# An mLSTM block and a rational feed-forward on one core: first gates by themselves, constants ahead of the branch, a new order of the work, the last step in halves

## The chip, the cores and the metric

The kernel runs on one core of one Trainium2 chip. The metric is the device time of one execution in microseconds (us). Lower is better.

## The reference

Two stages follow each other. The first is an mLSTM over 4 batches, 8 heads, 768 tokens and a head dimension of 40; the second sends the 3072 rows of 320 values through a feed-forward with 2048 hidden values and a rational activation. All inputs are 32-bit floats except the weights, which reach the device as 64-bit floats.

```python
for t in range(S):                       # S = 768
    m_new  = max(f_gate[t] + m, i_gate[t])
    f_stab = exp(f_gate[t] + m - m_new)
    i_stab = exp(i_gate[t] - m_new);  m = m_new
    C = f_stab * C + i_stab * outer(v[t], k[t])
    n = f_stab * n + i_stab * k[t]
    y[t] = sigmoid(o_gate[t]) * (C @ q[t]) / max(abs(n @ q[t]), 1)
h = x @ w_in                             # x = y, tokens by 320
P = a0 + a1*h + a2*h**2 + a3*h**3
Q = 1 + abs(b0)*abs(h) + abs(b1)*h**2
out = (P / (Q + 1e-6)) @ w_out
```

## The kernel before, in words

**Branch.** `_can_square` (line 233) loads the four numbers `moe_a`, decides on VectorE (DVE) whether the cubic can be written with a square, and reads the answer into registers. `tc.If` then runs one of two copies of `_program`. Here it is the copy with `square=True`.

**Gates.** `gates()` loads all of `f_gate` and `i_gate` (32 rows of 768), finds the running maximum with one scan, subtracts it, computes the exponential with 14 DVE instructions on tiles of 128x384, and multiplies the forget gates up in chunks of 64 tokens. The results go to DRAM: `scrF` (the gates themselves) and `scrA` (their products). Both are written in four quarters of three chunks each (`store_f`, `store_a`, lines 420 to 432), the first quarter at once and the other three when the order says so. The input gates are turned by TensorE (PE) into `inat`.

**Attention.** `attention(u)` handles unit u, 128 tokens of one batch: unit u has block n = u // 4 and batch b = u % 4. Units 0 to 3 are the first 128 tokens of the four batches, unit 4 the next 128 of batch 0. There are 24. A unit loads k and q (`ld`: tiles kr, qn), v (`lv`: vb) and its gates, spread over 64 partitions (`lg`: fb from scrF, ab from scrA). Its chain is: kp (k by gates, GpSimd, called POOL), tk and tq (transposes into kq on PE, copied by ScalarE, called ACT, to kT and qb), sc (the scan e on DVE), qA and P (pm, on DVE), then on PE S (ps), ow, it and i1 (y), then na, gt, xn, and a transpose px that ACT and DVE split into a high and a low part, xk.

**Weights.** w_in comes in eight slabs i0 to i7 and two slabs j0, j1, w_out in eight slabs o0 to o7. `split64` turns 64-bit floats into two 32-bit parts. Each slab needs two ACT passes (raw, z), two DVE passes (raw, z), a high part on ACT and a subtraction on POOL (wi, wo, wY).

**Feed-forward.** `feed_forward(n, i)`: two units make a block n of 256 tokens (12 blocks); step i of 8 handles 256 hidden values. f1 (16 matmuls into ph), then ha, u and p on ACT, w = w*ha on POOL, p on DVE, y and r0 on ACT, gH and m (w) on DVE, rm (p - w) on POOL, gL on DVE, and on PE f2 (gH by wo, 8 matmuls) and f3 (gL by wo, 4 matmuls) into the two tiles po. Step 7 of a block ends with two evictions ot and their DMAs to the output.

**Order.** Nothing is issued where it is written. Every operation is put into `_Plan` with a key, a cost, what it reads and what it writes; `_Plan.order()` plays the list forward and, on each engine, takes the ready operation with the smallest key. The keys come from the tables `FFN_AT`, `ATT_AT`, `PREP_AT`, `SLAB_AT` and others. `_Ordered` then ties each engine to that order, and all DMAs go through SyncE's (SP) queue. Instructions of one engine run in this order and wait at the head of the queue. `busy()` adds 90 matmuls `hot` whose result nobody reads.

Since nearly every instruction is issued by the recording helper at line 33, the trace is read by tiles (ps, y, po) rather than by lines.

## Time and profile before

| what | value |
|---|---|
| three timed runs | 578.12 us median, 577.51 to 578.72 |
| profiled execution, its own time | 580.5 us |
| span of that execution, first to last instruction | 578.6 us |
| granted TensorE clock, mean over the span | 0.957 of full |
| PE busy | 520.7 us (90%), 180 of its matmul rows are `hot` |
| DVE busy | 465.1 us (80%) |
| ACT busy | 430.6 us (74%) |
| POOL busy | 380.8 us (66%) |
| chain that ended last | PE 69%, DVE 5%, ACT 4% |

The table averages over stages with different limits. The timeline in 40 slices shows PE busy at nine tenths or more from the eleventh slice to the thirty-eighth, and mostly at less in the ten slices before; so the views by stage matter more than the shares. The profiled execution took 580.5 us, 1.9 us above its span and 2.4 us above the median of the timed runs.

### The profile page before, as it was taken

How to read it: one execution, taken by the hardware profiler on the slowest of the kernel's cores; microseconds unless marked ns; L12 is line 12 of the kernel's file. 1: busy time of each engine (PE TensorE's matmuls, PEld its weight loads, DVE VectorE, ACT ScalarE, POOL GpSimd, SP SyncE). 2: the span in 40 equal slices, each digit the busy share in tenths (PEclk: the TensorE clock that was granted, in tenths of full speed). 3: DMA queues.
4: the chain of work that ended last, by engine and by line, in shares of the span. 5: the costliest groups of instructions: out<-in, count | busy, mean ns of one | idle time of the engine just before them, and what ended most of it. 6: DMA issues, size and time to landing. Idle time of an engine off the chain costs nothing.

```text
span 578.6 us, 13044 instructions
## 1 busy us (share of the span) xinstructions
PE 520.7 (90%) x5023; PEld 488.8 (84%) x5023; DVE 465.1 (80%) x753; ACT 430.6 (74%) x751; POOL 380.8 (66%) x350
## 2 busy tenths in 40 slices
...
GB/s 91 309 177 174 240 216 147 93 66 48 77 77 49 83 65 62 85 63 56 80 54 65 84 42 84 76 53 72 53 49 44 6 1 24 1 24 2 23 1 30
DMA packets 120521, 44.06 MB, mean 76 GB/s; under 512 B 103746, under 2 KB 112962, under 8 KB 120450
## 3 DMA queue, kind: packets, MB, share of 16 engines
...
q14 instruction: 30, 0.25, 0.1%
...
## 4 chain that ended last, share of the span: by engine, by line
PE 69%; DVE 5%; ACT 4%; issue 2%; POOL 1%; DVEq 0%; ACTq 0%; POOLq 0%
PE ph L33 27%; PE po L33 26%; PE y L33 6%; PE ps L33 4%; PE kq L33 3%; PE ow L33 2%; PE px L33 2%; ACT ph L33 1%; DVE w L33 1%; DVE gH L33 1%; POOL p L33 1%; DVE gL L33 1%; DVE p L33 1%; ACT p L33 1%; ACT kT L33 0%
## 5 line engine op out<-in xcount | busy, mean ns | idle before, releaser
L33 POOL TENSOR_TENSOR p<-p,w 128x512 f32<-128x512 f32 x96 | 127.1, 1324 | 113.4 <-DVE w L33 108.0
L33 PE MATMUL ph<-xk,wi 128*128 128x256 f32 x1152 | 174.3, 286 | 1.7 <-DVE gL L33 1.7
L33 PEld LDWEIGHTS ph<-xk,wi 128*128 128x128 f32 x1152 | 152.6, 189 | 4.4 <-issue 2.3
L33 POOL TENSOR_TENSOR w<-w,ha 128x512 f32<-128x512 f32 x96 | 131.2, 1368 | 13.9 <-ACT w L33 12.8
L33 PE MATMUL po<-wo,gH 128*128 128x320 f32 x768 | 140.0, 318 | 0.0
L33 PEld LDWEIGHTS po<-wo,gH 128*128 128x128 f32 x768 | 115.4, 190 | 4.8 <-issue 2.7
L33 DVE SCALAR_TENSOR_TENSOR gH<-p,ps,ph 128x512 fp32r<-128x512 f32 x96 | 71.2, 741 | 24.8 <-ACT ph L33 19.8
L33 DVE SCALAR_TENSOR_TENSOR gL<-p,ps,ph 128x512 fp32r<-128x512 f32 x96 | 70.4, 733 | 24.6 <-POOL p L33 23.8
L33 DVE SCALAR_TENSOR_TENSOR w<-w,gH 128x512 f32<-128x512 f32 x96 | 81.4, 847 | 4.4
L33 ACT ACTIVATE w<-ha,ba 128x512 f32<-128x512 f32 x96 | 78.1, 814 | 6.2
L33 ACT ACTIVATE ph<-w,cd 128x512 f32<-128x512 f32 x96 | 66.0, 688 | 18.0 <-DVE p L33 11.2
L33 ACT ACTIVATE ha<-ph 128x512 f32<-128x512 f32 x96 | 57.2, 596 | 29.1 <-PE ph L33 29.0
L33 PE MATMUL po<-wo,gL 128*128 128x320 f32 x384 | 73.7, 313 | 4.2 <-DVE gL L33 4.1
L33 DVE SCALAR_TENSOR_TENSOR p<-p,ps,ph 128x512 f32<-128x512 f32 x96 | 71.0, 741 | 3.1 <-ACT p L33 2.1
L33 PEld LDWEIGHTS po<-wo,gL 128*128 128x128 f32 x384 | 60.0, 189 | 7.4 <-DVE gL L33 6.8
L33 ACT ACTIVATE p<-ph,ps 128x512 f32<-128x512 f32 x96 | 65.3, 680 | 0.3
L33 ACT ACTIVATE ph<-ph 128x512 f32<-128x512 f32 x96 | 55.9, 582 | 3.0
L33 PE MATMUL ph<-xk,wj 128*128 128x256 f32 x192 | 54.1, 282 | 0.0
L33 PE MATMUL ph<-xk,wY 128*128 128x256 f32 x192 | 54.0, 281 | 0.0
L33 DVE TENSOR_TENSOR_SCAN e<-fb,eye 128x512 f32<-128x512 f32 x24 | 40.8, 1699 | 0.2
L33 PE MATMUL ps<-qb,kT 104*64 104x128 f32 x384 | 28.9, 298 | 10.9 <-DVE qA L33 10.3
L33 PEld LDWEIGHTS ph<-xk,wj 128*128 128x128 f32 x192 | 36.5, 190 | 0.0
(108 smaller groups left out, 762.1 us busy)
## 6 DMA issues: line engine op xcount, KB each, us to landing
...
```

The lines of the kernel that those rows point to most:

```text
L33: made = fn(*args, **kwargs)
```

## The change

**Ahead of the branch.** A new `_prologue` makes the constants that both copies need (identity, `cd`, the cleared kp, qn0, vb0 and qb) and loads the gates of the first 128 tokens of all 32 rows (`ef`, `ei`, 32x128) before the answer of the branch is known.

**First gates.** A new `early()` repeats the gate computation on these 128 tokens: 27 instructions on DVE, one transpose on PE, two copies on ACT, and three DMAs into chunks 0 and 1 of scrF and scrA. Units 0 to 3 wait for these alone (`=scrF`, `=scrA`, `=inat0`). The large `gates()` still runs over all 768 tokens; its key is now `GATE_AT`, its first quarter stores only chunk 2, and `spread` leaves out the first column block.

**Last step.** With `HALVED = 1` the activation work of the very last step (block 11, step 7) is done in two halves of 256 columns each, and the second of the last two evictions runs on DVE.

**Order.** All tables are new, each operation can have its own offset (`NUDGE`, some 620 entries), and the planner's engines start at 3.6 to 4.1 us rather than 0.6 to 2.0. The first 24 `hot` matmuls have a cost of 0.45 instead of 0.22, and the first waits for the early gates' subtraction rather than for a point inside the large exponential.

```diff
+def _prologue(ctx, tc, args):
+    c = {name: pool.tile(shape, F32, name=name) for name, shape in (
+        ("ident", [P, P]), ("cd", [P, 1]), ("kp", [P, H, L]), ("qn0", [P, H, L]), ("vb0", [P, H, 2, D + 1]),
+        ("qb", [D + L, H // 2, 2, 2, L]), ("ef", [BH, 2 * L]), ("ei", [BH, 2 * L]),
+    )}
+    c["flag"] = _can_square(ctx, tc, args[8])
+    for t, src in ((c["ef"], args[4]), (c["ei"], args[3])):
+        nc.sync.dma_start(t, src.rearrange("b h s -> (b h) s")[:, 0 : 2 * L])
+    nc.vector.memset(c["kp"], 0.0)
+    nc.vector.memset(c["vb0"], 0.0)
+    make_identity(nc, c["ident"])
+    nc.gpsimd.memset(c["cd"], CD)
+    nc.gpsimd.memset(c["qn0"], 0.0)
+    nc.gpsimd.memset(c["qb"], 0.0)
+    return c
...
+    def early():
+        step(clear, 0.13, w=["em", "ep"], new=new)
+        step(lambda: V.tensor_tensor_scan(m[:, 1:], ef, ei, -1e30, op0=ALU.add, op1=ALU.max), 0.35, w=["em"])
+        step(lambda: V.tensor_tensor(f, ef, m[:, 0:C], ALU.add), 0.2, w=["em"])
+        step(less, 0.37, r=["em"], w=["ex.f", "ex.i", "mark"])
+        exp(
+            lambda fn, r, w, **kw: step(fn, r=["ex.f", "ex.i", "ep"], w=["ex.f", "ex.i", "ep"], **kw),
+            dict(gx=x, gt=t, gm=mm, gr=r, gp=p),
+        )
+        step(turn, 0.12, "PE", r=["ex.i"], w=["pe"], new=[("pe", ("a", 1))])
+        step(spread, 0.37, "ACT", r=["pe"], w=["inat0"])
+        step(firsts, 0.13, w=["ex.f", "ep"])
+        step(lambda: V.tensor_tensor_scan(a, x[:, 0:L], a0, 0.0, op0=ALU.mult, op1=ALU.add), 0.2, r=["ex.f"], w=["ep"])
+        plan.add("gate", FIRST - 1, "SP", 0.5, store_f, r=["ex.f"], w=["scrF"], lag=2.1)
+        plan.add("gate", FIRST - 1, "SP", 1.0, store_a, r=["ep"], w=["scrA"], lag=2.1)
...
-            key = FIRST - 1 if j == 0 else STORE_AT + j
+            key = STORE_AT + j
...
-        scr = [f"=scr{j}" for j in sorted({2 * n // CQ, (2 * n + 1) // CQ})]
+        scr = [f"=scr{j}" for j in sorted({2 * n // CQ, (2 * n + 1) // CQ})] if n else ["=scrF", "=scrA"]
...
+        last = NS * n + i >= NS * NU // 2 - HALVED
+        cuts = [slice(j * T, (j + 1) * T) for j in range(2)] if last else [slice(0, W)]
...
-        def f_w():
-            nc.gpsimd.tensor_tensor(d["w"], d["w"], d["ha"], op=ALU.mult)
+        def f_w(c):
+            nc.gpsimd.tensor_tensor(d["w"][:, c], d["w"][:, c], d["ha"][:, c], op=ALU.mult)
...
+            if engine == "DVE":
+                nc.vector.tensor_scalar(ot, po, pa[:, 3:4] if square else 1.0, None, op0=ALU.mult)
```

In the table of offsets a row reads like `S_0=40.63, ke_0=-15.75, P_0=11.71, ow_0=914.85`, one number for each operation of each unit or step.

**What the order does, first place: SP and PE from the branch to unit 0.** Names carry the unit or slab: kr0 is unit 0's k, rawi2 slab i2. On SP before, from the first load after the branch (unit 0's v, k and q stand ahead of the weights):

```order
L388 DMA gate_f_148<-in_f_gate_dram 32x768
L389 DMA gate_i_149<-in_i_gate_dram 32x768
L392 DMA pa_107<-in_moe_a_dram 128x4
L393 DMA pb_108<-in_moe_b_dram 128x2
L636 DMA vb0_118<-in_v_dram 64x8x40 x2
L630 DMA kr0_185<-in_k_dram 128x8x40
L631 DMA qn0_115<-in_q_dram 128x8x40
L630 DMA kr1_189<-in_k_dram 128x8x40
L528 DMA rawj0_200<-in_moe_w_in_dram 64x1024
```

On SP now, some rows after the branch:

```order
L720 DMA rawi2_215<-in_moe_w_in_dram 128x2x512
L720 DMA rawo0_225<-in_moe_w_out_dram 128x2x640
L528 DMA scrF_133<-early_kT_168 64x64
L532 DMA scrA_134<-early_qA_169 32x64 x2
L720 DMA rawi1_253<-in_moe_w_in_dram 128x2x512
L837 DMA fb0_265<-scrF_133 64x512 x2
L843 DMA ab0_266<-scrA_134 64x2x256 x2
L1077 DMA og0_285<-in_o_gate_dram 128x8x40
L837 DMA fb1_289<-scrF_133 64x512 x2
L843 DMA ab1_290<-scrA_134 64x2x256 x2
L1077 DMA og1_310<-in_o_gate_dram 128x8x40
L822 DMA kr0_315<-in_k_dram 128x8x40
```

The first gates are now written behind one j slab, two i slabs and one o slab, where before eight slabs had been issued; unit 0's k and q stand behind them, and its v (vb0) twelve rows further down, behind j1, i3, o3 and o1. On PE now, the first rows after the branch:

```order
L34 MATMUL hot_194<-ident_58 128x128 x11
L34 MATMUL pe_232<-ident_58,early_kT_168 64x64
L34 MATMUL hot_194<-ident_58 128x128 x59
L34 MATMUL kq0_396<-ident_58,kp_60 104x128 x4
L34 MATMUL hot_194<-ident_58 128x128 x8
L34 MATMUL kq0_424<-ident_58,qn0_61 104x128 x4
L34 MATMUL hot_194<-ident_58 128x128 x12
L34 MATMUL ow_0_476<-vb0_62,pm0_410 40x82 x8
L34 MATMUL ps_0_513<-qb_63,kT0_413 64x128 x8
```

All 90 `hot` matmuls now stand ahead of unit 0's ow; before, they were spread out down to unit 2's.

**Second place: DVE around P of unit 4**, the first unit that needs the large gates (pm4 is P, e4 the scan, p0_1 step 1 of block 0). Before:

```order
L33 TENSOR_TENSOR qA4_1028<-kq4_1010,ab4_963 104x512
L33 SCALAR_TENSOR_TENSOR e4_1036<-fb4_962,eye_106 128x512
L33 SCALAR_TENSOR_TENSOR zi5_1038<-zi5_1038,rawi5_722 128x512
L33 SCALAR_TENSOR_TENSOR zo5_1051<-zo5_1051,rawo5_796 128x640
L33 SCALAR_TENSOR_TENSOR rawi7_832<-rawi7_832 128x512
L33 TENSOR_TENSOR pm4_1065<-ps_4_1040,e4_1036 128x8x64
```

Now, with what follows it:

```order
L34 SCALAR_TENSOR_TENSOR e4_1027<-fb4_920,eye_127 128x512
L34 SCALAR_TENSOR_TENSOR zo5_1036<-zo5_1036,rawo5_703 128x640
L34 TENSOR_TENSOR qA4_1054<-kq4_1029,ab4_921 104x512
L34 TENSOR_TENSOR xn3_1064<-y_3_944,gt3_1034 128x320
L34 SCALAR_TENSOR_TENSOR p0_1_1062<-p0_1_1062,ps_130,ph0_1_876 128x512
L34 SCALAR_TENSOR_TENSOR zi7_1076<-zi7_1076,rawi7_809 128x512
L34 TENSOR_TENSOR pm4_1052<-ps_4_1067,e4_1027 128x8x64
L34 SCALAR_TENSOR_TENSOR p0_2_1079<-p0_2_1079,ps_130,ph0_2_926 128x512
L34 SCALAR_TENSOR_TENSOR e5_1104<-fb5_976,eye_127 128x512
L34 TENSOR_TENSOR sm_141<-tm4_0_1081,ow_4_1095 40x4x41 x2
L34 SCALAR_TENSOR_TENSOR gL0_0_1129<-p0_0_885,ps_130,ph0_0_830 128x512
```

In both orders 33 weight passes stand on DVE ahead of pm4; step 0's gL has moved behind it and step 1's p ahead of it. On PE, f3 of step 0 and f1 of step 3 have moved from ahead of unit 4's y to behind it.

**Third place: the end of POOL**, the last products of block 11 (w11_7 is w = w*ha of the last step, p11_6 and p11_7 the subtractions rm of the last two). Before:

```order
L33 TENSOR_TENSOR w11_6_7276<-w11_6_7276,ha11_6_7267 128x512
L33 TENSOR_TENSOR p11_5_7259<-p11_5_7259,w11_5_7247 128x512
L33 TENSOR_TENSOR w11_7_7338<-w11_7_7338,ha11_7_7325 128x512
L33 TENSOR_TENSOR p11_6_7283<-p11_6_7283,w11_6_7276 128x512
L33 TENSOR_TENSOR p11_7_7341<-p11_7_7341,w11_7_7338 128x512
```

Now:

```order
L34 TENSOR_TENSOR p11_5_7301<-p11_5_7301,w11_5_7289 128x512
L34 TENSOR_TENSOR w11_7_7376<-w11_7_7376,ha11_7_7371 128x256
L34 TENSOR_TENSOR p11_6_7325<-p11_6_7325,w11_6_7318 128x512
L34 TENSOR_TENSOR w11_7_7376<-w11_7_7376,ha11_7_7371 128x256
L34 TENSOR_TENSOR p11_7_7382<-p11_7_7382,w11_7_7376 128x256 x2
```

The subtraction of step 6 now stands between the two halves of the last w.

## Rows read from the trace of the kernel before

**Rows 1.** Busy time by stage: start:end, length, busy of each engine (instructions), PEclk, DMA.
```profile
4.00:100.00 96.00, 62.25 (x615) 55.92 (x615) 77.61 (x127) 59.81 (x108) 55.66 (x58) 0.85 0.89 203
100.00:111.00 11.00, 6.20 (x71) 5.30 (x72) 6.70 (x12) 7.04 (x14) 7.80 (x8) 0.50 0.49 102
117.00:540.00 423.00, 418.70 (x4114) 396.23 (x4113) 350.82 (x572) 336.39 (x587) 294.33 (x264) 1.00 0.24 53
```

**Rows 2.** Timeline of PE: start, us, what, [idle before <-releaser].
```profile
48.73 1.09 PE L33 MATMUL ps<-qb,kT 104*64 104x128 f32 x16
...
92.06 1.97 PE L33 MATMUL ps<-qb,kT 104*64 104x128 f32 x16 [5.62 <-DVE qA L33]
100.05 1.93 PE L33 MATMUL y<-vb,pm 128*64 128x41 f32 x32 [6.01 <-DVE pm L33]
...
105.87 1.06 PE L33 MATMUL kq<-ident,kp 128*104 128x128 f32 x4 [0.66 <-DVE st L33]
110.52 1.10 PE L33 MATMUL kq<-ident,qn 128*104 128x128 f32 x4 [3.58 <-ACT kT L33]
111.26 2.48 PE L33 MATMUL po<-wo,gH 128*128 128x320 f32 x8
```

**Rows 3.** Timeline of SP: issues after the branch, the last weight slab, unit 4's gates.
```profile
3.83 0.34 SPq L388 DMA_DIRECT2D gate_f<-in_f_gate_dram  x1
...
21.57 0.36 SPq L422 DMA_DIRECT2D scrF<-gate_w  x1
...
30.75 1.12 SPq L645 DMA_DIRECT2D fb<-scrF  x2
...
76.99 0.54 SPq L528 DMA_DIRECT2D rawo<-in_moe_w_out_dram  x1
...
85.52 1.18 SPq L645 DMA_DIRECT2D fb<-scrF  x2
```

**Rows 4.** Timeline of DVE and of POOL: waits and a long scan.
```profile
13.17 0.36 DVE L33 TENSOR_SCALAR gate_w<-gate_w 128x384 f32<-128x384 f32 x1 [1.58 <-POOL gate_w L33]
...
68.73 0.69 DVE L33 TENSOR_TENSOR qA<-kq,ab 104x512 f32<-104x512 f32 x1 [5.02 <-ACT qb L33]
...
91.31 0.69 DVE L33 TENSOR_TENSOR qA<-kq,ab 104x512 f32<-104x512 f32 x1 [2.21 <-DMA ab<-scrA]
91.92 3.94 DVE L33 TENSOR_TENSOR_SCAN e<-fb,eye 128x512 f32<-128x512 f32 x1
```

**Rows 5.** Groups of DVE instructions in the first 112 us: count, busy us, mean ns.
```profile
L33 DVE TENSOR_TENSOR_SCAN e<-fb,eye 128x512 f32<-128x512 f32 x6 | 11.8, 1958 | 0.1
L33 DVE SCALAR_TENSOR_TENSOR zo<-zo,rawo 128x640 int32<-128x640 int32 x7 | 8.3, 1199 | 0.0
L33 DVE SCALAR_TENSOR_TENSOR gate_gL<-gate_gL,gate_gH 128x384 f32<-128x384 f32 x5 | 2.8, 558 | 0.2
L33 DVE MEMSET vb<- 128x656 f32 x1 | 0.6, 605 | 0.1
L33 DVE MEMSET kp<- 128x512 f32 x1 | 0.5, 485 | 0.9 <-DVE flag_out L247 0.9
L33 DVE SCALAR_TENSOR_TENSOR ba<-pb 128x2 f32<-128x2 f32 x1 | 0.2, 153 | 0.0
```

**Rows 6.** Timeline of ACT: a slab's load ahead of unit 3's qb.
```profile
66.84 0.79 ACT L33 ACTIVATE rawo<-rawo 128x640 int32<-128x640 uint8 x1 [3.38 <-DMA rawo<-in_moe_w_out_dram]
```

**Rows 7.** Timeline of the last 9 us, all engines.
```profile
563.88 1.77 POOL L33 TENSOR_TENSOR w<-w,ha 128x512 f32<-128x512 f32 x1
...
569.14 1.27 POOL L33 TENSOR_TENSOR p<-p,w 128x512 f32<-128x512 f32 x1 [2.24 <-DVE w L33]
570.45 0.75 DVE L33 SCALAR_TENSOR_TENSOR gL<-p,ps,ph 128x512 fp32r<-128x512 f32 x1 [1.38 <-POOL p L33]
571.25 0.85 PE L33 MATMUL po<-wo,gL 128*128 128x320 f32 x4 [1.41 <-DVE gL L33]
572.00 0.95 ACT L33 ACTIVATE ot<-po,pa 128x320 f32<-128x320 f32 x2 [4.76 <-PE po L33]
```

More of the change, by code (lines that the diff above doesn't have):

```diff
@@ L192 @@
+GATE_AT = -33.56
+HOT_AT = 9.05
 COLD = 0
-STORE_AT = 143.81
-START = dict(DVE=0.6, ACT=1.6, POOL=0.8, PE=2.0, SP=0.6)
+STORE_AT = 85.52
+START = dict(DVE=4.1, ACT=4.0, POOL=3.6, PE=4.1, SP=3.8)
 BUFS = dict(fb=2, kr=2, ha=2, w=3, p=3, gH=2, gL=2, ot=2, z=4)
@@ L240, in _can_square, with decide, _decide @@
     tc.nc.sync.dma_start(a, moe_a.unsqueeze(0))
+    def decide():
+        return _decide(tc, a, b, t, out)
+    return decide
+def _decide(tc, a, b, t, out):
+    V = tc.nc.vector
     V.scalar_tensor_tensor(b, a, -1.0, a, op0=ALU.mult, op1=ALU.max)
@@ L349, in exp @@
                 lambda c=c: V.scalar_tensor_tensor(p, p, c, r, op0=ALU.add, op1=ALU.mult), r=[gr],
-                w=[gp, *(["mark"] if c == POLY[2] else [])],
+                w=[gp],
             )
@@ L384, in step @@
         def step(fn, cost=0.59, engine="DVE", w=(), r=(), **kw):
-            plan.add("gate", FIRST - 1, engine, cost, fn, r=r, w=w, **kw)
+            plan.add("gate", GATE_AT, engine, cost, fn, r=r, w=w, **kw)
         def load():
@@ L485, in setup, with ones @@
     def setup():
[L486 to L489 removed]
+        def ones(engine, t):
             for c in range(2):
[L491 to L492 removed]
+                engine.memset(t[c * L : (c + 1) * L, :, c, D], 1.0)
         def clear(engine, t):
             engine.memset(t, 0.0)
[L496 to L503 removed]
+            if t is vb[1]:
+                ones(engine, t)
+        plan.add("zero", FIRST - 2, "DVE", 0.25, lambda: ones(nc.vector, vb[0]), w=["vb0"])
+        later = [("qn1", qn[1], 0.5), ("vb1", vb[1], 0.8), ("sm", sm, 0.3)]
         later += [(f"st{j}", t, 0.3) for j, t in enumerate(st)]
@@ L995, in feed_forward, with add, own, each @@
         k = f"{n}_{i}"
-        hh, ha, w, p, gH, gL = (f"{x}{k}" for x in ("h", "ha", "w", "p", "gH", "gL"))
-        def add(name, engine, cost, fn, r=(), w=(), new=(), at=0.0, **kw):
-            plan.add(f"{name}_{k}", base + FFN_AT[name] + at, engine, cost, fn, r, [*w, f"turn {name}"], new, **kw)
+        a0, a1 = (ps[:, 2:3], ps[:, 1:2]) if square else (pa[:, 0:1], pa[:, 1:2])
+        def add(name, engine, cost, fn, r=(), w=(), new=(), at=0.0, part=None, **kw):
+            def own(x):
+                if x not in ("h", "ha", "w", "p", "gH", "gL"):
+                    return x
+                return f"{x}{k}" if part is None or not last else f"{x}{k}.{part}"
+            plan.add(
+                f"{name}{'half' if last and part is not None else ''}_{k}", base + FFN_AT[name] + at, engine, cost, fn,
+                [own(x) for x in r], [*(own(x) for x in w), f"turn {name}"],
+                [(f"{x}{k}" if x in BUFS or x == "h" else x, t) for x, t in new], **kw,
+            )
+        def each(name, engine, cost, fn, r=(), w=(), tag=None):
+            cost = COST.get(name, cost)
+            for j, c in enumerate(cuts):
+                add(
+                    name, engine, cost * 0.6 if last else cost, lambda c=c: fn(c), r, w,
+                    [(tag, (tag, BUFS[tag]))] if tag and j == 0 else (), at=0.1 * j, part=j,
+                )
         for j in range(2):
```

331 lines of the change are left out of this document (232 added, 99 removed).

## The prediction, made before the changed kernel ran

> **What bounds the kernel now.** I read the busy times by stage first. From 117 to 540 us PE is busy for 418.7 of 423 us at a granted clock of 1.00 [rows 1]: in this stretch PE is the bound, and nothing that another engine does faster there can show in the end. The change leaves PE's useful matmuls as they are in number and size. So a gain can only come from ahead of 117 us, or from behind 540, and whatever moves the start of the full stretch forward arrives at the end almost whole.
>
> Ahead of it stands a long start. From 4 to 100 us DVE is busy for 77.6 of 96 us, ACT for 59.8, and the DMA engines at a mean share of 0.89, while PE's 62.3 us hold the warming matmuls too [rows 1]. PE's own timeline shows what the start waits for: ps of unit 4 after 5.62 us of idling, y of unit 4 after 6.01 us, released by pm on DVE, then a second kq after 3.58 us for kT from ACT, and only at 111.26 us f2 of step 1, behind which PE no longer stops [rows 2]. So the mark to follow is P of unit 4 (pm4): it ended about 100.0 us, y began at 100.05. What made it late is seen on two engines. SP issued the last weight slab at 77.0 us and unit 4's gates at 85.5 [rows 3]; qA of unit 4 then waited for ab and ran at 91.31. But behind that DVE still needed 8 us: the scan took 3.94 us [rows 4] where its mean is 1.96 [rows 5], and three weight passes stood ahead of P. DVE work and DVE waits both count, so I make the sum on DVE.
>
> **The sum on DVE up to pm4.** Both orders put the same 33 weight passes, five scans and four units ahead of pm4; step 0's gL has left and step 1's p has come (gL takes 0.75 us, p much the same) [rows 7]. That part stays at the 77.6 us of before.
> - Removed: clearing kp, qn0 and vb. kp and vb measured 0.485 and 0.605 us [rows 5]; qn0 has kp's shape. Together 1.6 us. They now run while the branch waits for its four numbers, or on POOL; the answer came by way of seven small DVE instructions and SP's first issue after it stood at 3.83 us [rows 3]. I cost the prologue at nothing. Should DVE reach the decision late for its two memsets, the price is at most their 1.1 us.
> - Added: 27 instructions of the early gates. None is in the trace at this size. From below, 27 at the 0.153 us of a two-column instruction are 4.1 us. From above, at the 0.558 us of the 384-column one for the nine that are of its kind [rows 5] and the 0.36 us of the TENSOR_SCALAR [rows 4] for the other 18, they are 11.5 us. With 128 columns they are nearer to the small end, since a third of the columns remains: I take 6.5 us.
> - DVE idle: 18.4 us of the 96 (96.0 - 77.6) [rows 1]. Of this the rows show 1.58 us for POOL's subtraction, 2.21 for unit 4's ab and 5.02 for qb of unit 3 [rows 4], and that qb stood behind a slab pass for which ACT had waited 3.38 us [rows 6]. In the new order the large gates are threaded between weight passes, so the 1.58 us goes; the first gates are written behind four slabs and no longer behind eight, where 9.2 us passed from the issue of scrF at 21.57 to the first fb at 30.75 [rows 3]. What is late next is a slab: ACT still has slab loads ahead of kT and qb, unit 0's v stands behind nine slabs, and unit 0 itself may come no earlier than before. I keep 5 us, the one wait of that kind that the rows show; the ends are 0 and the 18.4 of before.
>
> So pm4 ends at 4.1 + 77.6 - 1.6 + 6.5 + 5 = 91.6 us instead of 100.0. The ends are 84.2 (4.1 us of early gates, no idling) and 110.0 (11.5 and 18.4).
>
> Can the DMA engines follow? Unit 4's fb stands behind all 18 slabs in both orders. They were busy for 0.89 of 96 us, 85 us [rows 1], so packed without a pause the same bytes are through some 10 us earlier, and ab of unit 4, which let qA go at 91.31, could land near 81. The forecast needs it by about 88. That holds if a third of the pauses goes.
>
> **From pm4 to f2 of step 1.** Before, 11.3 us (100.0 to 111.26), with both kq of unit 5 and the 3.58 us wait for kT inside. Now these kq stand behind f2, and eight DVE instructions stand from pm4 to gH of step 1: a scan (1.96), a zo pass (1.20) [rows 5] and six of at most 0.75 us (gL's duration) [rows 7], 7.7 us, and the hop to PE, 7.9 in all. f3 of step 0 and f1 of step 3, moved from ahead of y4 to behind it, fit into these 7.9 us: PE has nothing else. So f2 of step 1 starts at 99.5 instead of 111.26, 11.8 us earlier; the two kq that it owes cost 1.06 + 1.10 us at half clock, about 1.2 at full by the ratio of the two ps (1.97 to 1.09) [rows 2]. Net 10.6 us.
>
> **The tail.** The last w on POOL starts at 563.88 and takes 1.77 us, then the chain of step 7 goes on to f3 at 571.25 and two evictions on ACT, 0.95 us [rows 7]. Now rm of step 6 stands between the halves of w: 0.88 + 1.27 + 0.65 puts the second half's end at 566.7, 1.05 us later than the whole w. The 5.6 us from w's end to f3 (571.25 - 565.65) shrink to between one half and all of it, since hops and fixed parts don't halve; I take 0.6, 3.4 us. f3's second half takes 0.43 of 0.85. That ends at 570.5 instead of 572.1, 1.6 us, and 0.45 more for evictions on two engines: 2.0 us. The ends are a loss of 0.6 (factor 1) and a gain of 2.6.
>
> **The sum.** 10.6 + 2.0 = 12.6 us. The profiled execution took 580.5 us, so 567.9 by its time; it lies 2.4 us above the median of the runs shown, 578.1, from which the forecast is **565.5 us**. Against the many new offsets in the middle I set nothing: PE idles for 4.3 of 423 us there [rows 1], which is all that could be won, and with PE's queue full a new order that keeps it full loses nothing.
>
> **Rivals.**
> 1. *DVE never waits.* All slabs land before ACT asks. pm4 ends at 84.2, 7.4 us ahead of the forecast: 558 us. For it: the early DVE order has weight passes to fill every pause. Against it: DMA at 0.89 already. Chance 0.18.
> 2. *The clock stays at half.* All 90 warming matmuls now run ahead of unit 0's ow. In the rows PE's granted clock was 0.50 from 100 to 111 us [rows 1], the level of 1.2 GHz of 2.4, after idling for 5.62 and 6.01 us, and ps took 1.97 instead of 1.09 us [rows 2]. If every unit up to the fourth runs so, ps, y and two kq (6.06 us) cost 2.7 us more a unit, 13.5 over five, all in the chain: pm4 at 105.1, f2 at 113.0, and with the owed 1.2 and the tail's 2.0 the end is 1 us later: 579, no change or barely slower. Against it: DVE has other work while PE is slow, so only part of this is in the way. Chance 0.09.
> The Trainium skill, page "TensorE: Matmul & The Clock Gate", section "What's actually happening", states that the throttled clock is the default and that activity releases it, which speaks against spending the warming matmuls so early; the trace agrees (0.50 in the idle stretch, 1.00 in the full one). By that rule rival 2 would be the rule of the start; by the rows, only what lies in the chain counts.
> 3. *Slabs block ACT (slower).* ACT meets eleven slab loads between unit 0's kT and unit 4's qb, in order. At the 3.38 us that one of them cost [rows 6], eight that wait make 27 us of idling in place of 5: pm4 at 113.6, f2 at 121.5, 10.2 us late, plus 1.2, minus 2.0: 587.5 us. It decides for slower from 18 us of waits on, about five such loads. For it: v, k and q now stand behind slabs too. Against it: slabs are now issued from the first row behind the branch on, ahead of k, q and v. Chance 0.11.
>
> **How the numbers follow.** The forecast has 0.62; its own range, from early gates of 4.1 to 10, idling of 2 to 10 and the tail's ends, is 558 to 575. A measurement of this kernel can tell some 0.2%, 1.2 us. Faster: 0.62, 0.18 and a part of rival 2, 0.84. Within 0.2%: the rest of rival 2 but a little, 0.05. Slower: 0.11. The range of 8 in 10 goes from 554 (below rival 1, whose durations may shrink with less contention) to 577 and leaves out rivals 2 and 3.
>
> **What would show it.** Right: y of unit 4 on PE at 88 to 96 us, f2 of step 1 near 99, PE at 98% or more from there to the last block; DVE idle from 4 us to y of unit 4 for about 5 us; scrF first issued near 10 us; the last chain one POOL instruction longer but ending 2 us sooner after the last f1. Wrong: y of unit 4 behind 100 us; kT or qb waiting on ACT for slabs more than five times; a granted clock near 0.5 from 40 to 90 us with DVE idle behind ps; or PE under 97% between 150 and 540 us, which would mean that the new order is worse in the middle, where I cost it at nothing.

## The result, and the profile after

The changed kernel took 571.74 us (median of four runs, 570.24 to 573.32) beside 577.89 for the kernel before (577.51 to 578.72): a ratio of 0.9892, 95% interval 0.9862 to 0.9922. That is 6.2 us less, where 12.6 were forecast; the time lies inside the predicted range, which is 23 us wide. The profiled executions differ by 7.2 us in their spans (578.6 and 571.4), and four marks divide this difference:

| stretch | forecast, us | profiled, us |
|---|---|---|
| up to the end of pm4 | -8.4 (100.0 to 91.6) | -5.2 (100.0 to 94.83) |
| pm4 to the first f2 of step 1 | -3.4 (11.3 to 7.9) | -2.5 (11.26 to 8.81) |
| that f2 to the end of the last f1 | +1.2 | +1.1 (450.42 to 451.49) |
| end of the last f1 to the end of the last f3 | -2.0, with the next row | -0.2 (10.42 to 10.26) |
| end of the last f3 to the end of the span | | -0.5 (6.5 to 6.0) |

Busy time by stage, the changed kernel, with the columns of [rows 1]:

```profile
4.00:100.00 96.00, 71.67 (x661) 64.36 (x662) 86.35 (x153) 64.94 (x117) 59.36 (x57) 0.79 0.88 205
100.00:111.00 11.00, 9.09 (x77) 8.06 (x75) 10.18 (x16) 9.06 (x17) 10.00 (x8) 1.00 0.54 110
117.00:540.00 423.00, 417.15 (x4085) 393.84 (x4080) 351.67 (x569) 333.72 (x584) 301.32 (x264) 1.00 0.24 53
```

From 100 to 111 us PE is now at work at the full clock, 9.09 us where it was 6.20. In the long middle it is still the bound (98.6% busy). Up to 100 us DVE is busy for 86.35 of 96 us instead of 77.61: the start is fuller on DVE, not emptier. The DMA share, 0.88, is as it was.

PE's timeline, against [rows 2]:

```profile
51.26 1.93 PE L34 MATMUL y<-vb,pm 128*64 128x41 f32 x32 [1.30 <-DVE pm L34]
...
96.01 1.91 PE L34 MATMUL y<-vb,pm 128*64 128x41 f32 x32
...
103.64 1.44 PE L34 MATMUL po<-wo,gH 128*128 128x320 f32 x8 [1.20 <-DVE gH L34]
105.11 0.61 PE L34 MATMUL kq<-ident,kp 128*104 128x128 f32 x4
```

y of unit 4 comes at 96.01 instead of 100.05, f2 of step 1 at 103.64 instead of 111.26, and the two owed kq stand behind it, as the order said. But y of unit 0 comes at 51.26, which is 9 us later than before (its P began at 41.38 then and at 50.52 now). ACT shows one wait in its way, a case like [rows 6]:

```profile
37.80 0.65 ACT L34 ACTIVATE rawj<-rawj 128x512 int32<-128x512 uint8 x1 [7.36 <-DMA rawj<-in_moe_w_in_dram]
38.36 0.57 ACT L34 COPY kT<-kq 104x512 f32<-104x512 f32 x1
```

kT of unit 0 stood behind a slab for which ACT waited 7.36 us. SP's queue, against [rows 3], shows that slab's issue only at 30.68, behind the o gates of the first units:

```profile
12.74 0.48 SPq L528 DMA_DIRECT2D scrF<-early_kT  x1
...
16.83 1.10 SPq L837 DMA_DIRECT2D fb<-scrF  x2
...
27.77 2.86 SPq L1077 DMA_DIRECT2D og<-in_o_gate_dram  x3
30.68 1.57 SPq L720 DMA_DIRECT2D rawj<-in_moe_w_in_dram  x2
...
79.88 0.58 SPq L720 DMA_DIRECT2D rawo<-in_moe_w_out_dram  x1
80.56 1.48 SPq L837 DMA_DIRECT2D fb<-scrF  x2
```

The early gates (25 instructions on DVE, not the 27 that were counted) bring the first fb forward from 30.75 to 16.83 us, 14 us, and unit 0 comes no sooner for it. DVE's timeline and POOL's, against [rows 4], show the other half of the story:

```profile
5.74 3.18 DVE L34 TENSOR_SCALAR early_kT<-early_kT 64x128 f32<-64x128 f32 x2
...
60.74 3.47 DVE L34 SCALAR_TENSOR_TENSOR rawi<-rawi 128x512 int32<-128x512 int32 x1
64.14 0.68 DVE L34 TENSOR_TENSOR pm<-ps,e 128x512 f32<-128x512 f32 x1
```

```profile
5.68 1.30 POOL L34 MEMSET st<- 104x328 f32 x4
7.04 1.80 POOL L34 MEMSET wY<- 64x2048 f32 x1
...
59.37 1.55 POOL L34 TENSOR_TENSOR wo<-zo,wo 128x640 fp32r<-128x640 f32 x1
60.88 1.29 POOL L34 TENSOR_TENSOR wi<-zi,wi 128x512 fp32r<-128x512 f32 x1
62.13 1.54 POOL L34 TENSOR_TENSOR wo<-zo,wo 128x640 fp32r<-128x640 f32 x1
```

Two small instructions of the early gates take 3.18 us and end just after POOL's clearing of wY does (8.92 and 8.84). A weight pass that elsewhere in this trace takes 0.69 us takes 3.47 while three subtractions follow each other on POOL, and it ends 0.54 us after the third. P, which reads PSUM, takes 0.68 to 0.69 us every time.

The end of the last step, all engines, against [rows 7] (ph <- w is y in the kernel's words; the x2 is both halves of p):

```profile
557.28 1.22 DVE L34 SCALAR_TENSOR_TENSOR w<-w,gH 128x512 f32<-128x512 f32 x1
...
558.42 0.73 DVE L34 SCALAR_TENSOR_TENSOR gL<-p,ps,ph 128x512 fp32r<-128x512 f32 x1
...
559.08 0.86 DVE L34 SCALAR_TENSOR_TENSOR p<-p,ps,ph 128x256 f32<-128x256 f32 x2
...
560.04 0.48 ACT L34 ACTIVATE ph<-w,cd 128x256 f32<-128x256 f32 x1 [1.63 <-DVE p L34]
...
561.52 0.48 ACT L34 ACTIVATE ph<-w,cd 128x256 f32<-128x256 f32 x1 [0.61 <-DVE gH L34]
```

The first half of y waits 1.63 us until DVE is through with *both* halves of p; the second waits for gH of the first. The halves do not overlap as the forecast had it.

### The profile page after: what moved, and what is told of

It reads as the page before. It is cut to its first block, busy times and chain, and to the rows that moved or that the text cites. A ratio compares the mean times of both kernels' runs of the same rounds, so it can differ in the third digit from the quotient of the medians.

```text
span 571.4 us, 13096 instructions
## 1 busy us (share of the span) xinstructions
PE 526.4 (92%) x5024; PEld 492.9 (86%) x5024; DVE 475.8 (83%) x782; ACT 430.8 (75%) x757; POOL 394.3 (69%) x353
## 4 chain that ended last, share of the span: by engine, by line
PE 68%; DVE 11%; POOL 6%; issue 4%; DMA 3%; ACT 3%; SPq 3%; DVEq 0%; POOLq 0%; ACTq 0%
PE ph L34 27%; PE po L34 25%; PE y L34 6%; PE ps L34 4%; PE kq L34 3%; PE ow L34 2%; DVE w L34 2%; DVE gH L34 2%; POOL p L34 2%; DVE gL L34 1%; ACT ph L34 1%; POOL tm L34 1%; PE px L34 1%; DMA rawj<-in_moe_w_in_dram 1%; DMA rawo<-in_moe_w_out_dram 1%
## 5 line engine op out<-in xcount | busy, mean ns | idle before, releaser
L34 POOL TENSOR_TENSOR p<-p,w 128x512 f32<-128x512 f32 (+1 forms) x97 | 128.7, 1327 | 85.0 <-DVE w L34 78.3
L34 POOL TENSOR_TENSOR w<-w,ha 128x512 f32<-128x512 f32 (+1 forms) x97 | 138.4, 1427 | 34.9 <-ACT w L34 31.0
L34 DVE SCALAR_TENSOR_TENSOR gH<-p,ps,ph 128x512 fp32r<-128x512 f32 (+1 forms) x97 | 71.6, 738 | 34.0 <-PE po L34 15.3
L34 DVE SCALAR_TENSOR_TENSOR w<-w,gH 128x512 f32<-128x512 f32 (+1 forms) x97 | 84.3, 870 | 5.7 <-POOL p L34 0.5
L34 ACT ACTIVATE ha<-ph 128x512 f32<-128x512 f32 (+1 forms) x97 | 57.4, 592 | 40.6 <-PE ph L34 40.4
L34 ACT ACTIVATE w<-ha,ba 128x512 f32<-128x512 f32 (+1 forms) x97 | 78.7, 811 | 4.8 <-POOL p L34 0.4
L34 ACT ACTIVATE ph<-w,cd 128x512 f32<-128x512 f32 (+1 forms) x97 | 66.2, 683 | 20.3 <-DVE p L34 14.4
L34 DVE SCALAR_TENSOR_TENSOR gL<-p,ps,ph 128x512 fp32r<-128x512 f32 (+1 forms) x97 | 71.3, 735 | 10.4 <-POOL p L34 8.8
L34 DVE SCALAR_TENSOR_TENSOR p<-p,ps,ph 128x512 f32<-128x512 f32 (+1 forms) x97 | 71.0, 736 | 4.3 <-ACT p L34 3.4
L34 ACT ACTIVATE p<-ph,ps 128x512 f32<-128x512 f32 (+1 forms) x97 | 65.4, 674 | 0.9 <-DVE gL L34 0.7
```

What stands on the lines that cost most here:

```text
L34: made = fn(*args, **kwargs)
```

## The experiments

Fourteen profiles lie behind this section, and one caution comes first. The changed kernel, profiled twice, gave pm4 starting at 94.14 and at 91.95 us, and f2 of step 1 at 103.64 and at 102.07. Three of the kernels below (last step whole, reordered, in two tiles) have the same order up to the last step; with them, five profiles of one start put pm4 between 91.95 and 94.44. Two more kernels that share another start are 3.3 us apart (90.18 and 93.48). So a mark of the start is good to some 3 us and the length from the first f2 of step 1 to the last f1 to some 1.3 us (451.4 to 452.7 in the five), while the length from the last f1 to the last f3 repeats to a few hundredths. Where a run says something about the start, its median counts first. Each ratio is to the kernel before, timed again beside that run with medians of 576.75 to 577.68 us, so runs are compared by their ratios.

| run | median, us | ratio to before, 95% interval | pm4 starts | f2 of step 1 | last f1 to last f3 |
|---|---|---|---|---|---|
| after, second time | 571.91 | 0.9891, 0.9865 to 0.9918 | 91.95 | 102.07 | 10.26 |
| before + prologue alone | 577.86 | 1.0003, 0.9986 to 1.002 | 96.40 | 108.35 | 10.42 |
| last step whole | 571.43 | 0.9904, 0.9876 to 0.9932 | 94.44 | 104.33 | 10.44 |
| no early gates | 572.23 | 0.9897, 0.9869 to 0.9924 | 94.11 | 103.62 | 10.27 |
| no early gates, units fed sooner | 576.03 | 0.9982, 0.9964 to 0.9999 | 97.80 | 107.75 | 10.26 |
| slab j1 behind kT | 570.77 | 0.9887, 0.9867 to 0.9907 | 92.88 | 102.39 | 10.26 |
| clearings later | 570.22 | 0.9884, 0.9866 to 0.9903 | 90.18 | 100.05 | 10.26 |
| subtractions on DVE | 575.50 | 0.9978, 0.9959 to 0.9998 | 96.50 | 105.66 | 10.27 |
| last step reordered | 571.46 | 0.9892, 0.9867 to 0.9917 | 92.33 | 101.83 | 10.69 |
| last step in two PSUM tiles | 569.23 | 0.9865, 0.9839 to 0.9891 | 93.38 | 102.88 | 8.37 |
| three edits together | 573.42 | 0.9934, 0.9913 to 0.9956 | 93.48 | 101.55 | 8.39 |
| the same, slabs sooner | 574.82 | 0.9950, 0.9928 to 0.9972 | 96.17 | 106.25 | 8.35 |

In the diffs, MOVES is a list of pairs: the first operation is put behind the second on its own engine ("<" puts it ahead of it), and nothing else in that engine's order changes. Of a slab, raw is the load, s0 and s1 the first passes on ACT and DVE, o0 the high part on ACT; of a unit, ld and lv are the loads of k with q and of v, lg and ogl its gates' loads, ek and eq kT and qb, P pm; of a step, gh, gl, m and rm are gH, gL, m and rm. All runs compute the whole output.

### The control, and the prologue alone

The changed kernel once more, with no edit:

> The changed kernel once more, nothing edited, so that the pieces can be set against it on one chip. Its first measurement was 571.74 us, 0.9892 of before; the same again is expected, 0.989 plus or minus 0.002.

571.91 us: the result repeats. Then the kernel before with the new prologue (without its loads of the first gates) and nothing else:

```diff
+        common = _prologue(ctx, tc, args)
+        flag = common.pop("flag")()
-            _program(tc, True, *args)
+            _program(tc, True, common, *args)
...
-    kp = cp.tile([P, H, L], F32, name="kp")
+    kp, qb = common["kp"], common["qb"]
...
-            engine.memset(t, 0.0)
+            if not any(t is x for x in common.values()):
+                engine.memset(t, 0.0)
```

> The kernel before, with only the prologue of the change: kp, vb of unit 0, qn of unit 0 and qb are cleared ahead of the branch, the identity and CD are made there, everything else stays in its order. The forecast took 1.6 us of DVE work off for it. Theory: all of DVE's work ahead of P of unit 4 counts, so P of unit 4 ends 1 to 2 us earlier and the time is 1 to 2 us lower, 575.5 to 576.5 us on this chip. Rival: DVE waits for 18.4 us in that stretch, for slabs and gates that come no earlier, so the 1.6 us are lost in the waits: within 0.5 us of the kernel before.

577.86 us, no change (at most 0.2% either way by the interval). The 1.6 us of clearings that leave DVE bought nothing in the old order. In its profile pm4 stands 2.9 us ahead of the one of before (96.40 for 99.31) with the same median, so part of the 5.2 us in the table of the result may be such scatter too.

### The last step whole

```diff
-HALVED = 1
+HALVED = 0
```

> The changed kernel with step 7 of the last block whole again (the eviction on two engines stays). The forecast's tail term says halves and the second engine give 2.0 us together, of which 0.45 stay here, so this is 1.5 us slower than the changed kernel: 573.3 us against its 571.7, and the stretch from the end of the last f1 to the end of the last f3 grows from 10.3 to 11.8 us. Theory now: the halves gave nothing, because the first half of y waited 1.63 us for both passes of p on DVE, which stand behind m and gL of steps 6 and 5; then the stretch stays at 10.3 plus or minus 0.3 and the time at 571.7 plus or minus 0.5.

10.44 us from the last f1 to the last f3, as in the kernel before (10.42), against 10.26 with the halves: they are worth 0.2 us. This kernel keeps the second eviction on DVE, and its span ended 6.1 us behind the last f3, where the other runs lie between 5.6 and 8.0, so the 0.45 us forecast for that eviction can't be told from the scatter.

### Why the halves gave nothing: order, or one tile

First the order of the tail alone, with w's second half ahead of rm of step 6 on POOL and p's first half ahead of m of step 6 on DVE:

```diff
+    ("whalf_11_7#1", "<rm_11_6#0"),
+    ("p3half_11_7#0", "<m_11_6#0"),
```

> The changed kernel with two instructions of the tail moved: on POOL the second half of the last w ahead of rm of step 6, on DVE the first half of the last p ahead of m of step 6. Theory: the first half of y (ACT) waited 1.63 us for p on DVE and not for POOL's rm, so it starts near 3 us after the last f1 and not 4.9, and the stretch from the end of the last f1 to the end of the last f3 shrinks from 10.3 to 8.6 us: 570.0 us, 1.5 less than the changed kernel. Rival 1, that y waits for both halves of p, as they lie in one tile: the stretch shrinks by 0.3 at most. Rival 2, rm of step 6 comes later by a half of w (0.74 us) and f3 of step 6 with it, and the end is held by that: within 0.5 us of the changed kernel.

The stretch became 10.69 us, no shorter. The second half of y had taken over the wait:

```profile
560.13 0.48 ACT L34 ACTIVATE ph<-w,cd 128x256 f32<-128x256 f32 x1 [1.48 <-DVE gH L34]
```

y writes its half of the PSUM tile ph, gH of the other half reads the same tile, and so the program orders them one behind the other. That gH was late besides, since on DVE gL of step 6 stood ahead of it and waited for POOL:

```profile
558.90 0.75 DVE L34 SCALAR_TENSOR_TENSOR gL<-p,ps,ph 128x512 fp32r<-128x512 f32 x1 [1.22 <-POOL p L34]
```

The next kernel gives each half a tile of its own, keeps the two moves, and puts gL of step 6 behind m's first half:

```diff
-            if j == 0:
-                d["h"] = psH.tile([P, W], F32, tag="h", name=f"ph{n}_{i}")
+            if j == 0 or last:
+                d["h"] = psH.tile([P, W], F32, tag="h", name=f"ph{n}_{i}" + f"_{j}" * last)
+                d[j * T] = d["h"]
...
-            nc.scalar.activation(d["h"][:, c], d["w"][:, c], AF.Abs_reciprocal_sqrt, bias=cd[:, 0:1])
+            nc.scalar.activation(ph(c)[:, c], d["w"][:, c], AF.Abs_reciprocal_sqrt, bias=cd[:, 0:1])
...
+    ("whalf_11_7#1", "<rm_11_6#0"),
+    ("p3half_11_7#0", "<m_11_6#0"),
+    ("gl_11_6#0", "mhalf_11_7#0"),
```

> The changed kernel with the two halves of the last step's ph in two PSUM tiles and not in two column ranges of one, and the order around them turned: second half of w ahead of rm of step 6 on POOL, first half of p ahead of m of step 6 and gL of step 6 behind the first half of m on DVE. Theory: the halves could not overlap since every instruction on the second half waited for the first half's last reader or writer in the one tile (y's second half waited 0.61 to 1.48 us for gH's first half). With two tiles y's halves run side by side with gH, and the stretch from the end of the last f1 to the end of the last f3 shrinks from 10.3 to 9.0 us (8.6 to 9.3). Rival, that the chain over four engines is as long in halves as whole, since an instruction on 256 columns takes 0.37 to 0.48 us where one on 512 takes 0.58 to 0.75, and every hop stays: 10.0 us or more. The time itself changes by 1.3 us at most, near what can be measured.

```profile
556.38 0.48 DVE L34 SCALAR_TENSOR_TENSOR p<-p,ps,ph 128x256 f32<-128x256 f32 x1
...
557.52 0.47 ACT L34 ACTIVATE ph<-w,cd 128x256 f32<-128x256 f32 x1
...
558.86 0.48 ACT L34 ACTIVATE ph<-w,cd 128x256 f32<-128x256 f32 x1 [0.47 <-DVE p L34]
...
562.41 0.88 PE L34 MATMUL po<-wo,gL 128*128 128x320 f32 x4
```

The first y no longer waits, the second waits 0.47 us for its own p, and the stretch is 8.37 us: 1.9 less than in the changed kernel, 2.3 less than with one tile and the first two moves. How much of this is the second tile and how much the move of gL is not separated: neither ran without the other. The stretch came out within 0.04 us of that in both later kernels with this tail. This is the fastest kernel of the study, 569.23 us (568.53 to 571.03); its interval against before overlaps that of the changed kernel, but the shorter tail is beyond the scatter.

### What POOL costs DVE

Six clearings on POOL, four of st among them, moved behind kp of unit 1:

```diff
+    ("zero#3", "kp_1#0"),
+    ("zero#4", "zero#3"),
...
+    ("zero#8", "zero#7"),
...
-            "zero", FIRST, "POOL", 2.0, lambda: nc.gpsimd.memset(wY[L:P].bitcast(F32), 0.0), w=["wj0", "wj1"]
+            "zero", FIRST, "POOL", 2.0, lambda: nc.gpsimd.memset(wY[L:P].bitcast(F32), 0.0), w=["wYz"]
```

> The changed kernel with six of POOL's clearings (sm, four st, the second half of wY) moved from ahead of the early gates to behind kp of unit 1, about 35.5 us, where POOL waits. Theory: DVE's TENSOR_SCALARs of the early gates stood behind POOL's clearings (3.18 us for two where the later ones take 0.22 each), so the early gates end at 10.3 us and not at 13.0, scrF is issued near 10.0 and not at 12.7, and since DVE's work bounds the start, P of unit 4 ends 1 to 2.7 us earlier: 569 to 571 us. Rival 1, the clearings only stand in another pass's way at 35 to 39 us: the early gates are shorter but P of unit 4 stays at 94.8 plus or minus 0.7, and the time at 571.7. Rival 2, the two TENSOR_SCALARs are long by themselves: they stay at 3.1 us and nothing moves.

```profile
5.74 0.47 DVE L34 TENSOR_SCALAR early_kT<-early_kT 64x128 f32<-64x128 f32 x2
```

The same two instructions take 0.47 us where they took 3.18, and scrF is issued at 10.04 instead of 12.74: the clearings held them, and without that the early chain takes 6.1 us (4.2 to 10.3), near the 6.5 forecast. That these 2.7 us reach the end is not shown: this run's median is 1.5 us below the changed kernel's, but by the ratios the two are 0.1% apart and the intervals overlap, and two later kernels with the same edit and the same 0.47 us had pm4 at 93.48 and 96.17.

The second test takes all the weights' low-part subtractions away from POOL:

```diff
-        nc.gpsimd.tensor_tensor(out, a, b.bitcast(F32), op=ALU.subtract)
+        nc.vector.tensor_tensor(out, a, b.bitcast(F32), op=ALU.subtract)
```

> The changed kernel with all subtractions that make the low parts of the weights on DVE, at the same place of the order, and none on POOL. Sixteen of them stand ahead of P of unit 4. Theory: DVE's SBUF-only passes stand still while POOL works on SBUF; 18 of DVE's 83 us up to P of unit 4 are such stretching, some 11 to 13 us of it beside these subtractions. Then DVE gains 16 x 0.7 = 11 us of work and loses about as much stretching: P of unit 4 at 94 plus or minus 3, time 568 to 576 us, and rawi, zi, rawo, zo are at 0.68 and 0.82 us nearly throughout. Rival, the stretching comes from something else (DMA writes into SBUF): the durations stay long and DVE has 11 us more, P of unit 4 near 106 us, time near 582.

Groups of DVE's instructions up to 97 us in this kernel, and then, up to 95 us, two rows of the changed kernel to hold against them (count, busy us, mean ns):

```profile
L34 DVE SCALAR_TENSOR_TENSOR rawi<-rawi 128x512 int32<-128x512 int32 x8 | 5.5, 684 | 0.0
L34 DVE TENSOR_TENSOR wi<-zi,wi 128x512 fp32r<-128x512 f32 x7 | 4.8, 679 | 0.3 <-ACT wi L34 0.3
L34 DVE TENSOR_TENSOR wo<-zo,wo 128x640 fp32r<-128x640 f32 x5 | 4.1, 825 | 0.1
...
L34 DVE TENSOR_TENSOR wY<-zj,wj 64x512 fp32r<-64x512 f32 x4 | 3.1, 784 | 0.1
...
L34 DVE SCALAR_TENSOR_TENSOR zj<-zj,rawj 128x512 int32<-128x512 int32 x2 | 1.4, 685 | 0.0
```

```profile
L34 DVE SCALAR_TENSOR_TENSOR rawi<-rawi 128x512 int32<-128x512 int32 x8 | 9.2, 1148 | 0.6 <-ACT rawi L34 0.6
...
L34 DVE SCALAR_TENSOR_TENSOR zj<-zj,rawj 128x512 int32<-128x512 int32 x2 | 2.7, 1358 | 0.0
```

DVE took on 12.0 us of subtractions (4.8 + 4.1 + 3.1), and yet from 4 us to the end of pm4 it was busy for 83.5 us, in the changed kernel 82.9 and 83.6. What came on was paid for by what no longer stretched: rawi fell from 1148 to 684 ns a pass, zj from 1358 to 685. Not all passes fell: rawo stayed at 1022 ns (1031 in the changed kernel), as POOL still had its other work. Without the subtractions 71.5 us are left, so of DVE's busy time in the start about a seventh is time in which it stands behind POOL's subtractions. The kernel is still slower than the changed one (575.5 us). The loss stands ahead of pm4, which starts at 96.50 with DVE idle for 9.7 us; from f2 of step 1 to the last f1 it takes 452.1 us, as the others do. What makes it wait there is not shown.

The Trainium skill, page "SBUF — State Buffer", section "SBUF: two separate sides", says that VectorE in a two-port mode, or with two SBUF inputs against a GpSimd operation that reads SBUF, and GpSimd lock one port pair for a whole instruction, and that the other then blocks. The trace agrees in kind: 0.69 us becomes 3.47, and P, with an operand in PSUM, stays at 0.68 to 0.69.

### Less work on DVE

Is DVE's sum the bound of the start? The early gates are left out, the large ones run in one piece in front and write all chunks, and their loads and those of units 0 and 1 are moved along:

```diff
+    ("gate#2", "<raw_j0#0"),
+    ("gate#3", "gate#2"),
+    ("gate#4", "early#21"),
...
+    ("raw_j1#0", "raw_i1#0"),
+    ("ogl_0#0", "raw_j1#0"),
+    ("ogl_1#0", "ogl_0#0"),
+    ("ld_0#0", "ogl_1#0"),
+    ("ld_1#0", "ld_0#0"),
...
-            plan.add("early", FIRST - 1, engine, 0.2 if cost > 0.38 else cost, fn, r=r, w=w, **kw)
+            plan.add("early", FIRST - 1, engine, 0.2 if cost > 0.38 else cost, lambda: None, r=r, w=w, **kw)
```

> The changed kernel without the early gates: the large gates stand in one piece at their place at the front on DVE (and hold the first 128 tokens too), as in the kernel before; the order of everything else stays, but for the loads of gate_f and gate_i in front, the first loads of k, q and o and slab j1 ahead of the stores of the gates. Theory (DVE's work ahead of P of unit 4 is the bound, and the early gates are 8.8 us of it): DVE loses 8.8 us of work and waits some 3.5 us for gate_f and gate_i at the start, so P of unit 4 ends 4 to 5 us earlier, near 90, and the time is near 566.5 (565 to 568). Rival (the forecast's reason: the first gates must be written early): the first fb comes near 27 instead of 17 us and the weight passes begin at 23.5 instead of 15.7, unit 0's y comes later than 52 and the time is 573 to 577 us.

572.23 us, the time of the changed kernel. DVE was busy for 72.0 of the 91 us up to 95 us, 11 less, and pm4 started at 94.11, where it was. The changed kernel, then this one, in the columns of [rows 1]:

```profile
4.00:95.00 91.00, 67.25 (x595) 60.11 (x597) 83.02 (x147) 60.01 (x108) 54.36 (x52) 0.79 0.89 209
```

```profile
4.00:95.00 91.00, 65.69 (x594) 59.54 (x596) 72.01 (x122) 59.62 (x106) 52.68 (x52) 0.79 0.89 209
```

The time turned into waits, on DVE and, behind them, on ACT and PE (4 to 95 us; us in total, times, longest). Those of DVE, then those of ACT:

```profile
DVE rawi L34 <- ACT rawi L34: 4.7, 1, 4.7
DVE rawo L34 <- ACT rawo L34: 3.2, 2, 2.1
DVE e L34 <- DMA fb<-scrF: 2.8, 1, 2.8
```

```profile
ACT rawi L34 <- DMA rawi<-in_moe_w_in_dram: 8.7, 6, 4.5
ACT rawo L34 <- DMA rawo<-in_moe_w_out_dram: 7.5, 3, 4.6
```

Now the slabs are late. The next kernel adds to this one an earlier v of units 0 and 1, slabs i3 and o3 sooner on SP, their kT and qb sooner on ACT, and their passes ahead of the weights on DVE:

```diff
+    ("lv_0#0", "ld_1#0"),
+    ("raw_i3#0", "lg_1#0"),
+    ("raw_o3#0", "raw_i3#0"),
+    ("lv_1#0", "raw_o3#0"),
+    ("eq_0#0", "o0_i0#0"),
...
+    ("P_0#0", "qa_0#0"),
...
+    ("ek_1#0", "ab_0#0"),
```

> The kernel without the early gates, with its queues turned to use what DVE won: v of units 0 and 1 and slabs i3 and o3 stand further forward on SP, qb of unit 0 and kT and qb of unit 1 further forward on ACT, and on DVE qA, P, sm, st and the scan of units 0 and 1 stand ahead of the weight passes of slabs i3 to o2. Without the early gates DVE idled for some 22 of 91 us, and unit 0 waited 7.5 us for its v. Theory now (DVE's work is the bound only as long as the queues bring what it asks for; the early gates are work that could be left out): P of unit 0 comes near 40 us and not at 50.7, and P of unit 4 at 86 to 90 and not at 94.1; time 564 to 568 us. Rival (the DMA engines are the bound: 0.89 of the stage, above 1 from 30 to 51 us): the slabs come no earlier, DVE waits for them instead, P of unit 4 stays at 92 to 96 and the time at 570 to 573.

576.03 us, 4 slower. Unit 0's P began at 40.05, ten microseconds sooner, and unit 4's at 97.80, later: DVE's busy time fell to 67.15 of 91 us, and from 51 to 66 us it was

```profile
51.00:66.00 15.00, 6.19 (x59) 4.97 (x58) 8.58 (x14) 10.86 (x20) 10.98 (x10) 0.50 1.15 291
```

8.58 of 15, with the DMA engines at their highest share of any stage in that kernel. What was asked for sooner seems to have held up what came behind it; no run separates the moves.

The wait of 7.36 us ahead of unit 0's kT was tried by itself: j1's first pass on ACT goes behind kT and wi, its pass on DVE behind the last gate.

```diff
+    ("s0_j1#0", "o0_i0#0"),
+    ("s1_j1#0", "gate#28"),
+    ("s1_i3#0", "s1_j1#0"),
```

> The changed kernel with the first pass of slab j1 on ACT moved behind kT and wi, and on DVE its pass and that of slab i3 behind the last of the large gates. Theory (DVE's work and waits add up): ACT's wait of 7.36 us at 30.4 us is no longer ahead of kT of unit 0, kT runs near 31 and not at 38.4, DVE's idle 2.59 us at 35.9 is filled with gates, and P of unit 4 ends 2 to 3 us earlier: 569 us (568.7 to 570). Rival 1, that the order behind it (unit 0's ow waits for v at 45.0, qA stands behind seven passes) holds everything: kT early but unit 0's y still at 51 and P of unit 4 within 0.7 of 94.8, 571.7. Rival 2, another slab is waited for in its place (i3 or o3 on ACT): DVE idles 2 us or more elsewhere, same time or slower.

```profile
42.51 1.32 PE L34 MATMUL ow<-vb,pm 128*40 128x82 f32 x16 [7.33 <-DMA vb<-in_v_dram]
```

7.36 us of waiting on ACT became 7.33 us of waiting on PE, for v of the same unit; 570.77 us, not told apart from the changed kernel. In the five profiles of the unedited start ACT's wait for j1 is 4.71 to 7.36 us, and the two longest go with the two latest pm4.

### Three edits together

To see whether the pieces add up: the later clearings, the two-tile tail, and a third that had not run alone. Here the sigmoids of og of units 6 to 9 go behind qb of unit 5 on ACT, and gH of step 1 ahead of gL of step 0 on DVE:

```diff
+    ("r0_0_1#0", "y_0_1#0"),
+    ("og_6#0", "eq_5#0"),
+    ("gh_0_1#0", "<gl_0_0#0"),
```

> The kernel after the change with three edits together: the six clearings on POOL moved behind kp of unit 1, the sigmoids of og of units 6 to 9 moved behind qb of unit 5 on ACT with gH of step 1 ahead of gL of step 0 on DVE, and the last step's product in two PSUM tiles with its DVE and POOL work reordered. Theory (each edit takes what it alone took, and they lie one behind the other): last f1 to last f3 8.4 us instead of 10.3 (-1.9), the two TENSOR_SCALARs 0.5 instead of 3.2 us and with them pm of unit 4 up to 2 us earlier (-0.4 to -2), pm of unit 4 to the first f2 of step 1 about 7.6 instead of 8.8 (-1.2): 566.5 to 568.5, ratio about 0.982. Rival: the start is held by the arrival of the slabs, so that pm of unit 4 stays at 92 to 94; only the tail counts: 569.3, ratio 0.9865.

573.42 us: worse than the tail alone. The tail held (8.39 us) and f2 of step 1 came 7.4 us behind pm4 instead of 8.8, as expected. But from that f2 to the last f1 it was 455.7 us, where the start's five profiles have 451.4 to 452.7. ACT, then DVE, around unit 5:

```profile
107.94 1.28 ACT L34 ACT_TABLE_LOAD   x1
109.24 1.55 ACT L34 ACTIVATE og<-og 128x320 f32<-128x320 f32 x4
110.70 0.77 ACT L34 ACTIVATE zo<-rawo 128x640 f32<-128x640 f32 x1
...
113.02 1.28 ACT L34 ACT_TABLE_LOAD   x1
```

```profile
111.50 0.85 DVE L34 SCALAR_TENSOR_TENSOR zo<-zo,rawo 128x640 int32<-128x640 int32 x1 [2.48 <-ACT zo L34]
112.28 0.73 DVE L34 SCALAR_TENSOR_TENSOR gL<-p,ps,ph 128x512 fp32r<-128x512 f32 x1
112.94 0.68 DVE L34 TENSOR_TENSOR pm<-ps,e 128x512 f32<-128x512 f32 x1
```

The two table loads and the sigmoids, 4.1 us (2 x 1.28 + 1.55), stand in ACT's way again: a weight pass on DVE waits 2.48 us for ACT, P of unit 5 waits behind that pass, and y of unit 5 starts at 119.08 instead of 117.05, 17.5 us behind that f2 where it was 13.4, which is as much as the stretch grew. The place they came from was the cheaper one.

The last kernel adds j1's moves and puts the o gates' loads of units 2 to 5 behind slab i4 on SP (the issue that stood ahead of slab j1 above), with the sigmoid that follows them behind qb of unit 2:

```diff
+    ("s0_j1#0", "o0_i0#0"),
...
+    ("ogl_2#0", "raw_i4#0"),
+    ("ogl_3#0", "ogl_2#0"),
...
+    ("og_2#0", "eq_2#0"),
```

> The kernel of the run before, and in it slab j1's passes put behind unit 0's kT on ACT and behind the last small gate on DVE, and the o-gate loads of units 2 to 5 moved on SP from ahead of slab j1 to behind slab i4, with their sigmoids behind qb of unit 2. Theory (slabs that are asked for sooner fill what DVE waits for them, about 5 us of idle up to pm of unit 4): pm of unit 4 1 to 2.5 us earlier than in the run before, 564.5 to 567.5, ratio about 0.979. Rival 1 (DVE's sum sets the end whatever comes sooner): the same as the run before. Rival 2 (v of unit 0 or the later o-gates hold the units, as where the feeding was moved before): slower than the run before by 1 to 4 us.

574.82 us. Units 0 and 1 came 2 to 3 us sooner than in the run before, units 3 and 4 about 3 later, no more than a start scatters. The theory of slabs that fill DVE's waits fell; between the rivals the interval, which overlaps that of the run before, does not decide.

## Why the prediction was right, and where it was not

**The bound was read rightly.** PE at 98% or more in the middle, the gain from ahead of 117 us, pm4 and f2 of step 1 as the marks: each shows in the profile after. The two kq paid back later fit less tightly than the table has it: +1.1 for +1.2 there, +1.0 to +2.3 over five profiles. The mechanism (less of the order ahead of pm4 waits, and what is not needed for it goes behind) fits what happened. But the gain is half of what was forecast, and a range of 554 to 577 leaves out little more than no change and slower. Three terms were mis-sized, and two reasons were wrong.

**"DVE idle ... I keep 5 us" (pm4 at 91.6): this step failed.** pm4 ended at 94.83, in the five profiles of this start at 92.6 to 95.1. The work in the sum was nearly right: 77.6 - 1.6 + 6.5 = 82.5 us, and DVE was busy for 82.9 up to the end of pm4. Idling was 8.0 us, in the five profiles 5.0 to 8.2. The deeper fault is the form, work plus a fixed idle time. Taking 11 us of work away left pm4 where it was, because idling grew by as much; asking sooner for the data of the first units made pm4 later. So DVE's work alone does not set the end. The likely other bound is the arrival of data in SP's order, but it is read from waits and no run isolates it: in 13 of the 14 profiles pm4 starts 12.5 to 15.2 us behind SP's issue of unit 4's fb (18.9 with the subtractions on DVE), and in the changed kernel this issue came 5.0 us sooner (80.56 for 85.52) and pm4 5.2. SP waits too: up to 100 us it stood for 10.7 us ahead of v loads until PE was through with y of an earlier unit.

**The prologue's -1.6 us was credited for nothing.** Alone, in the old order, it gives 0. The early gates, +6.5 us as costed, took 8.8 (4.2 to 13.0), 2.7 of it behind POOL's clearings. Leaving them out changes nothing, neither the cost nor the 14 us by which they bring fb forward. That the sum still came within 1 to 3.5 us of pm4 is in part luck: it holds these two terms, +4.9 us together, and neither moved pm4 when it was tried. So of the parts of the start, the order carries the gain; this follows by elimination, as the order's tables were not run by themselves, and which of its moves count stays open.

**"hop to PE, 7.9 in all": 8.81.** The duration of zo, 1.47 for 1.20, and two waits for POOL, 1.20 us for gL's p and 1.03 for st's tm, were not in it, while the scan took 1.37 for 1.96.

**The tail's factor "between one half and all of it; I take 0.6": it was 0.76.** From the end of the second half of w, at 560.56, to the last f3 piece, at 564.83, it took 4.27 us of the 5.6. That half of w also ended 1.46 us later than the whole w did, against 1.05 forecast (5.43 and 3.97 us behind the last f1). Halves gained 0.2 of the 1.6 us credited to them. The step took for granted that halves of one tile run beside each other; in this program they share the PSUM tile ph and follow one another. With two tiles and the order to match, the gain is 1.9 us, what the forecast had for the tail.

**The rivals.** DVE did not run without waits (rival 1); its 558 us would have needed slabs ahead of ACT, and ACT waited 7.36 us for one. Rival 2's clock appeared: granted 0.50 from 51 to 66 us, where it was 1.00 before. Its price did not: DVE waited for ps only 1.0 us in all up to pm4. In the five profiles of this start the clock of that stretch was 0.50, 0.61, 0.61, 0.73 and 0.50, and pm4, at 94.14, 91.95, 94.44, 92.33 and 93.38, does not follow it. No run changed the clock alone. Rival 3 struck once, at unit 0, and needed five.
